# Attention and gated MLP on one core: gate taken off TensorE, V load, gate-weight load and Q evictions moved, units cut finer

## Chip, cores and metric

One core of one Trainium2 chip. The time is device microseconds of one execution. Most numbers below are medians of several executions, with the spread. A run carries a state (fast or slow). For one core, slow means more than 1.5% above the fastest run of the same kernel. The profile shows one execution of each kernel, and its span is about 1.7 us shorter than the time of that execution.

## The reference, cut to what matters

```python
x = A_x                                              # 2048 x 512, bf16
g = sigmoid((x * gate_w).sum(-1, keepdims=True))     # one number per token
a = A_ref(x, wqkv, wo)      # 32 heads of 16, causal, sliding window of 256
b = B_ref(x, w1, w3, w2)    # (silu(x @ w1) * (x @ w3)) @ w2, inner size 1376
return g * a + (1 - g) * b
```

Both branches read the same `x`.

## The kernel before

The kernel builds a list of operations, each with an engine, an assumed duration and its dependencies. It then places them in time with a small list scheduler while the program is built. What runs on the chip is a fixed order of instructions on each engine. TensorE (PE) carries everything: the projections, the score bursts (four matmuls at once, 32 rows each, into a PSUM buffer "big" of which there is only one), the products with V (PV), the MLP ("up" and "down") and the output projection. ScalarE (ACT) does one exp per burst, GpSimd (POOL) masks it, and VectorE (DVE) evicts most of the rest.

```python
# loads: the ACT queue and the SP queue
dma("x0", "SP", 3.4, ...)      # 256 rows of x
dma("k0", "ACT", 3.4, ...)     # K weights of the first 8 heads
dma("x1", "SP", 4.2, ...)
dma("q0", "ACT", 4.2, ...)
dma("v", "ACT", 6.0, lambda: w_dma(nc.scalar, wqkv_sb, A_wqkv, 2 * D, 3 * D))   # 512 KB
dma("x2", "SP", 7.5, ...); dma("x3", "SP", 8.0, ...); dma("kq", "SP", 11.0, ...)
# ... w1, w3, the rest of x, w2, wo
nc.gpsimd.dma_start(out=gwc[:], in_=gate_w.rearrange("(c p) -> p c", p=P))      # 1 KB

# gate: 16 one-column matmuls for each quarter of the tokens
def pe():                                            # in add_gate
    b = bank(key)
    for j in range(4):
        m = 4 * m4 + j
        for dc in range(NDC):
            nc.tensor.matmul(b[:, j:j + 1], lhsT=xT[:, dc, m * P:(m + 1) * P],
                             rhs=gwc[:, dc:dc + 1], start=(dc == 0), stop=(dc == NDC - 1))

# Q eviction: one half on ACT, one on DVE
bs = [Op(("ACT",) if i == 0 else ("DVE",), d, evac_q(i), [a], rel=[("g", key)], rank=-0.5)
      for i in range(2)]

# units of PE work: parts of two matmuls; a burst can be put between parts
a0, a = pe_unit(0.87, [pe(kg, w1_sb, 0), pe(kg, w1_sb, 2)], ...)   # up; V, Q, K, output alike
cuts = [0, 2, 4, 6, 8, NFC]                                        # down: parts of 2, 2, 2, 2, 3

# the scheduler may run the MLP units only in their order
if o.kind == "ffn" and not o.cont and o.seq != ffn_next:
    continue
```

The softmax here doesn't subtract the row's maximum and nothing guards it: scores larger than these inputs give would overflow.

## Time and profile before

| | before |
|---|---|
| median of 16 runs | 273.68 us (270.59 to 274.86) |
| span of the profiled execution | 270.9 us |
| PE busy | 255.8 us, 94% |
| ACT, POOL, DVE busy | 204, 150, 141 us |
| PE waits | 1.4 us for exp, 3.6 us for the V weights, 4.0 us for transposes in the tail |

The page of the profile, first the busy time, then rows that cut the span into 40 slices (the clock in tenths, the bytes moved in GB/s):

```profile
PE 255.8 (94%) x2814; PEld 126.0 (47%) x2814; DVE 140.8 (52%) x248; ACT 204.4 (75%) x161; POOL 150.2 (55%) x251
...
PEclk9889999999999999999999999999999999999995
...
GB/s 146 343 208 269 301 6 7 13 11 13 12 5 17 10 7 7 10 12 10 12 10 12 13 4 9 10 13 10 13 9 12 47 46 30 48 31 50 39 56 45
```

All waits of PE (us in total, times, longest):

```profile
PE g L423 <- DMA OT<-ocur: 4.0, 3, 2.5
PE g L284 <- DMA wqkv_sb<-in_A_wqkv_dram: 3.6, 1, 3.6
PE big L472 <- ACT edm L480: 1.4, 3, 0.8
PE g L730 <- DVE scr L96: 1.3, 1, 1.3
PE g L198 <- DMA xs<-in_A_x_dram: 0.6, 2, 0.4
PE g L239 <- DVE h L361: 0.3, 1, 0.3
```

PE is the bound, and what it loses lies at the two ends. The Trainium skill, "Perfetto Trace Analysis", section "Identifying the Most-Contended Engine", warns that matmul busy time is a poor measure of the distance to the peak. The timeline of the head (start, duration, engine, line, operation) shows the gap:

```profile
1.37 0.87 POOL L159 DMA_DIRECT2D gwc<-in_gate_w_dram  x1 [0.32 <-issue]
...
6.04 1.73 PE L239 MATMUL g<-xT,wqkv_sb 128*128 128x256 bf16 x12
...
11.39 0.96 PE L284 MATMUL g<-wqkv_sb,xT 128*128 128x512 bf16 x2 [3.63 <-DMA wqkv_sb<-in_A_wqkv_dram]
...
12.29 0.61 PE L472 MATMUL big<-qz,kt 32*128 32x512 bf16 x4
```

PE does nothing from 7.77 to 11.39 us, and the first burst (L472) comes only after that. The same head as busy time in stretches (length, busy time of PE, PEld, DVE, ACT, POOL with counts, then granted clock, DMA share, GB/s):

```profile
4.00:6.00 2.00, 1.39 (x16) 1.17 (x17) 0.91 (x3) 0.00 (x0) 0.99 (x2) 1.00 0.85 196
6.00:8.00 2.00, 1.67 (x14) 1.06 (x11) 0.81 (x2) 1.68 (x3) 0.00 (x0) 1.00 0.88 275
8.00:11.00 3.00, 0.00 (x0) 0.00 (x0) 0.58 (x2) 0.28 (x1) 0.00 (x0) 1.00 1.10 349
11.00:15.00 4.00, 3.61 (x12) 1.02 (x13) 0.69 (x1) 1.88 (x1) 0.10 (x1) 0.57 1.51 319
```

After the gap the granted clock is 0.57 on average for four microseconds. The tail, PE's timeline without the PV matmuls:

```profile
254.16 0.39 PE L472 MATMUL big<-qz,kt 32*128 32x512 bf16 x4
256.61 0.29 PE L472 MATMUL big<-qz,kt 32*128 32x256 bf16 x4 [0.76 <-ACT edm L480]
...
258.88 1.04 PE L423 MATMUL g<-xs,OT 128*128 128x512 bf16 x4 [1.22 <-DMA OT<-ocur]
260.23 0.39 PE L423 MATMUL g<-xs,OT 128*128 128x512 bf16 x1 [0.31 <-DMA OT<-ocur]
...
264.96 2.31 PE L423 MATMUL g<-xs,OT 128*128 128x512 bf16 x5 [2.48 <-DMA OT<-ocur]
```

PE waits for the attention output to be normalised and transposed by DMA, and the last five matmuls run at half clock (0.46 us each).

### The profile page before, as it was taken

The page shows a single profiled execution, that of the slowest core. Times are in us where ns is not written, and L with a number is a line of the kernel's source. Part 1 is how long each engine was busy: PE and PEld are TensorE (multiplying, and loading weights), DVE is VectorE, ACT ScalarE, POOL GpSimd, SP SyncE. Part 2 cuts the span into 40 slices and gives each one's busy share as a digit, 9 for nine tenths or more (in the row PEclk, how much of TensorE's full clock was granted, in tenths as well). Part 3 has the DMA queues.
Part 4 walks back from the last instruction along what each step waited for, and adds up shares of the span by engine and source line. Part 5 has one row for each costly group of instructions (what it writes and reads, how often), then busy time and mean ns, then how long its engine had stood idle before and what let it go on. Part 6 is the DMA issues. An engine that isn't in the chain of part 4 may idle for free.

```text
span 270.9 us, 6643 instructions
## 1 busy us (share of the span) xinstructions
PE 255.8 (94%) x2814; PEld 126.0 (47%) x2814; DVE 140.8 (52%) x248; ACT 204.4 (75%) x161; POOL 150.2 (55%) x251
## 2 busy tenths in 40 slices
PE   7499999999999999999999999999999999999853
PEld 3154555445554545545554555544554454545420
DVE  1164775575565545554736545465554656544432
ACT  3278887896988887898878978899778778867600
POOL 5036656556645666465745755576655755575620
PEclk9889999999999999999999999999999999999995
DMA  5999900000000000000000000000000111111111
GB/s 146 343 208 269 301 6 7 13 11 13 12 5 17 10 7 7 10 12 10 12 10 12 13 4 9 10 13 10 13 9 12 47 46 30 48 31 50 39 56 45
DMA packets 24750, 13.05 MB, mean 48 GB/s; under 512 B 16176, under 2 KB 24720, under 8 KB 24720
## 3 DMA queue, kind: packets, MB, share of 16 engines
q1 hardware_dynamic: 23104, 11.84, 17.4%
q10 hardware_dynamic: 1584, 0.79, 1.0%
q8 instruction: 22, 0.36, 0.6%
q0 software_dynamic: 32, 0.00, 0.2%
q14 instruction: 8, 0.07, 0.1%
HBM read 7.37 MB, written 2.10 MB: 35 GB/s over the span
## 4 chain that ended last, share of the span: by engine, by line
PE 85%; DMA 5%; ACT 4%; DVE 2%; issue 1%; SPq 0%; ACTq 0%
PE g L349 27%; PE g L395 15%; PE g L535 13%; PE big L472 11%; PE g L239 10%; PE g L423 5%; PE g L284 5%; DMA wqkv_sb<-in_A_wqkv_dram 3%; ACT edm L480 3%; DMA OT<-ocur 2%; DVE qz L257 1%; ACT ef L480 1%; DVE h L361 1%; ACT tt L356 0%; SPq L550 0%
## 5 line engine op out<-in xcount | busy, mean ns | idle before, releaser
L480 ACT ACTIVATE edm<-big 128x2048 bf16<-128x2048 f32 x64 | 116.7, 1824 | 33.5 <-PE big L472 26.7
L489 POOL TENSOR_SCALAR_AFFINE_SELECT edm<-edm 128x512 bf16<-128x512 bf16 x128 | 78.6, 638 | 68.8 <-ACT edm L480 65.4
L494 POOL TENSOR_SCALAR_AFFINE_SELECT ef<-ef 128x512 bf16<-128x512 bf16 x112 | 67.6, 636 | 39.3 <-ACT ef L480 37.9
L349 PE MATMUL g<-xT,w_sb 128*128 128x512 bf16 (+1 forms) x352 | 86.2, 380 | 0.0
L480 ACT ACTIVATE ef<-big 128x2048 bf16<-128x2048 f32 x28 | 52.6, 1877 | 10.6 <-PE big L472 9.9
L361 DVE SCALAR_TENSOR_TENSOR h<-tt,g 128x512 bf16<-128x512 bf16 (+1 forms) x44 | 30.1, 684 | 40.1 <-ACT tt L356 39.9
L349 PEld LDWEIGHTS <-w_sb 128*128 128x128 bf16 (+1 forms) x352 | 31.7, 100 | 39.0 <-issue 7.9
L395 PE MATMUL g<-w_sb,hT 128*128 128x512 bf16 (+1 forms) x176 | 42.6, 380 | 0.0
L535 PE MATMUL g<-Vaug,edm 128*128 128x17 bf16 x992 | 41.0, 170 | 0.0
L535 PEld LDWEIGHTS <-edm 128*128 128x128 bf16 x992 | 38.5, 96 | 4.1
L472 PE MATMUL big<-qz,kt 32*128 32x512 bf16 (+1 forms) x480 | 36.2, 330 | 1.5 <-ACT edm L480 1.4
L535 PE MATMUL g<-Vaug,ef 128*128 128x17 bf16 x448 | 37.2, 171 | 0.0
L535 PEld LDWEIGHTS <-ef 128*128 128x128 bf16 x448 | 35.1, 96 | 4.4 <-issue 1.1
L239 PE MATMUL g<-xT,wqkv_sb 128*128 128x512 bf16 (+1 forms) x136 | 33.2, 367 | 0.4 <-DVE h L361 0.3
L367 DVE TENSOR_TENSOR hT<-h,g 128x512 bf16<-128x512 bf16 (+1 forms) x44 | 30.1, 685 | 4.0 <-PE g L349 1.2
L356 ACT ACTIVATE tt<-g 128x512 bf16<-128x512 f32 (+1 forms) x44 | 26.0, 592 | 0.4 <-PE g L349 0.4
L395 PEld LDWEIGHTS <-hT 128*128 128x128 bf16 (+1 forms) x176 | 15.7, 98 | 20.0 <-issue 3.6
L404 DVE TENSOR_SCALAR bsb<-g,omg 128x512 bf16<-128x512 f32 x16 | 12.0, 750 | 23.0 <-PE g L395 23.0
L472 PEld LDWEIGHTS <-kt 32*128 32x128 bf16 x480 | 10.2, 91 | 29.3 <-issue 28.3
L284 PE MATMUL g<-wqkv_sb,xT 128*128 128x512 bf16 x64 | 17.7, 405 | 3.7 <-DMA wqkv_sb<-in_A_wqkv_dram 3.6
L423 PE MATMUL g<-xs,OT 128*128 128x512 bf16 x64 | 17.1, 400 | 4.0 <-DMA OT<-ocur 4.0
L430 DVE SCALAR_TENSOR_TENSOR ot<-g,gq,bsb 128x512 bf16<-128x512 f32 x16 | 11.9, 749 | 12.6 <-PE g L423 12.1
(37 smaller groups left out, 116.7 us busy)
## 6 DMA issues: line engine op xcount, KB each, us to landing
out_dram<-ot SPq DMA_DIRECT2D x16, 128.0 KB, 1.7
w_sb<-in_B_w_dram SPq DMA_DIRECT2D x2, 864.0 KB, 7.0
w_sb<-in_B_w_dram SPq DMA_DIRECT2D x1, 1280.0 KB, 6.4
xs<-in_A_x_dram SPq DMA_DIRECT2D x4, 256.0 KB, 5.8
w_sb<-in_B_w_dram SPq DMA_DIRECT2D x2, 512.0 KB, 10.0
OT<-ocur SPq DMA_TRANSPOSE x64, 2.4
wqkv_sb<-in_A_wqkv_dram SPq DMA_DIRECT2D x2, 384.0 KB, 9.2
wqkv_sb<-in_A_wqkv_dram ACTq DMA_DIRECT2D x1, 512.0 KB, 9.4
```

Source lines behind the costliest of these rows:

```text
L239: nc.tensor.matmul(b[:, 0:n], lhsT=wqkv_sb[:, dc, col0:col0 + P], rhs=xT[:, dc, t0:t1], start=(dc == 0), stop=(dc == NDC - 1))
L284: nc.tensor.matmul(b[:], lhsT=xT[:, c, m * P:(m + 1) * P], rhs=wqkv_sb[:, c, 2 * D:3 * D], start=(c == 0), stop=(c == NDC - 1))
L349: nc.tensor.matmul(b[0:fs, :], lhsT=wsb[:, dc, f * P:f * P + fs], rhs=xT[:, dc, t * 512:(t + 1) * 512], start=(dc == 0), stop=(dc == NDC - 1))
L361: nc.vector.scalar_tensor_tensor(out=tl["h1"][0:fs, :], in0=tl["tt"][0:fs, :], scalar=1.0, in1=g_tile[kg][0:fs, :], op0=ALU.add, op1=ALU.mult)
L367: nc.vector.tensor_tensor(out=h_tile[t][0:fs, f, :], in0=tl["h1"][0:fs, :], in1=g_tile[ku][0:fs, :], op=ALU.mult)
L395: nc.tensor.matmul(b[:], lhsT=h_tile[t][0:fs, f, (m % 4) * P:(m % 4 + 1) * P], rhs=w2_sb[0:fs, f, :], start=(f == 0), stop=(f == NFC - 1))
L423: nc.tensor.matmul(b[:], lhsT=OT[:, c * S + m * P:c * S + (m + 1) * P], rhs=wo_t[c // 2][:, c % 2, :], start=(c == 0), stop=(c == NDC - 1))
L472: nc.tensor.matmul(big[:, u, k * 256:k * 256 + 2 * w], lhsT=kt[32 * u:32 * u + 32, kb * P:(kb + 1) * P], rhs=qz[32 * u:32 * u + 32, :, q0: ...
L480: nc.scalar.activation(out=e[:, :, 0:2 * n], in_=tl["big"][:, :, 0:2 * n], func=ACT.Exp, scale=SCALE)
L489: nc.gpsimd.affine_select(out=tri, in_=tri, pattern=[[0, 2], [0, 2], [1, P]], compare_op=ALU.is_ge, fill=0.0, base=0, channel_multiplier=-1)
L494: nc.gpsimd.affine_select(out=tri, in_=tri, pattern=[[0, 4], [-1, P]], compare_op=ALU.is_ge, fill=0.0, base=-1, channel_multiplier=1)
L535: nc.tensor.matmul(pva[:, k, h8, :], lhsT=lhsT, rhs=Vaug[:, kp, 8 * c + h8, :], start=(bi == 0), stop=(bi == len(blocks) - 1))
```

## The change

The intent: have the V weights early, take the gate off PE, take Q evictions off ACT, and cut units so finely that there is always filler for PE. Cut to its core:

```diff
-    dma("v", "ACT", 6.0, lambda: w_dma(nc.scalar, wqkv_sb, A_wqkv, 2 * D, 3 * D))
+    dma("v", "SP", 6.5, lambda: w_dma(nc.sync, wv_sb, A_wqkv, 0, D, 2 * D))    # between x1 and x2
+    # wv_sb lies in a sixth exp buffer, which is free for exp once V is done
-    nc.gpsimd.dma_start(out=gwc[:], in_=gate_w.rearrange("(c p) -> p c", p=P))
+            if o.eng == "POOL" and not gw_done:              # while the order is written out
+                npool[0] += 1
+                if npool[0] == 9:                            # before the ninth mask
+                    nc.gpsimd.dma_start(out=w1_sb[:, :, F:F + 1], in_=gate_w.rearrange("(c p x) -> p c x", p=P, x=1))
-    # 64 gate matmuls
+            m = fs + 1 if has_z and key == kg else fs        # last chunk of w1: row 97 is the gate
+        def put(eng):
+            nc.sync.dma_start(out=zd[t:t + 1, :], in_=tl["tt"][row:row + 1, :])   # row to DRAM
+        def get(eng):
+            nc.sync.dma_start(out=st["gt"][:], in_=zd[t, :].rearrange("(j p) -> p j", p=P))  # back, as columns
-            bs = [Op(("ACT",) if i == 0 else ("DVE",), d, evac_q(i), ...
+            bs = [Op("DVE", d, evac_q(i), ...
-        ... [pe(kg, w1_sb, 0), pe(kg, w1_sb, 2)] ...         # and all other units
+        ... [pe(kg, w1_sb, i) for i in range(NDC)] ...
-        cuts = [0, 2, 4, 6, 8, NFC]
+        cuts = range(NFC + 1)
```

Left out of this print: the weights of Q, K and V in three tiles, the transposes of x in halves evicted by DVE and ACT side by side, the last w1 chunk taken fifth, Q before K for the first 512 tokens, K's first eviction allowed on ACT, and new assumed landing times.

More of the change, by code (lines that the diff above doesn't have):

```diff
@@ L58 @@
     bsb = pp.tile([P, NT, D], BF16, name="bsb")
-    gwc = pp.tile([P, NDC], BF16, name="gwc")
-    w1_sb = pp.tile([P, NDC, F], BF16, name="w1_sb")
+    w1_sb = pp.tile([P, NDC, F + 1], BF16, name="w1_sb")
     w3_sb = pp.tile([P, NDC, F], BF16, name="w3_sb")
-    wqkv_sb = pp.tile([P, NDC, 3 * D], BF16, name="wqkv_sb")
+    wk_sb = pp.tile([P, NDC, D], BF16, name="wk_sb")
+    wq_sb = pp.tile([P, NDC, D], BF16, name="wq_sb")
     eo = pp.tile([P, 4], F32, name="eo")
@@ L70 @@
     smpool = ctx.enter_context(tc.tile_pool(name="sm", bufs=3))
+    dr = ctx.enter_context(tc.tile_pool(name="dr", bufs=1, space=bass.MemoryType.DRAM))
+    zd = dr.tile([NTC, 512], F32, name="zd")
     ps = ctx.enter_context(tc.tile_pool(name="ps", bufs=1, space=bass.MemoryType.PSUM))
@@ L90, in hold @@
         refs[(pool, key)] = n
+    hold("edm", "wv", NT)
+    slot_of[("edm", "wv")] = 5
     def slot(pool, key):
@@ L108, in xt_dma, with w_dma @@
                                     in_=x2d[512 * t:512 * (t + 1), c * P:(c + 1) * P])
-    def w_dma(eng, dst, src, lo, hi):
-        eng.dma_start(out=dst[:, :, lo:hi], in_=src[:, lo:hi].rearrange("(c p) f -> p c f", p=P))
+    def w_dma(eng, dst, src, lo, hi, base=0):
+        eng.dma_start(out=dst[:, :, lo:hi],
+                      in_=src[:, base + lo:base + hi].rearrange("(c p) f -> p c f", p=P))
+    wv_sb = sb.tile([P, NDC, D], BF16, name="edm5")
     land = {}
@@ L117, in dma @@
         land[name] = at
-    dma("x0", "SP", 3.4, lambda: x_dma(0, 0))
-    dma("k0", "ACT", 3.4, lambda: w_dma(nc.scalar, wqkv_sb, A_wqkv, D, D + P))
-    dma("x1", "SP", 4.2, lambda: x_dma(0, 1))
-    dma("q0", "ACT", 4.2, lambda: w_dma(nc.scalar, wqkv_sb, A_wqkv, 0, P))
-    dma("v", "ACT", 6.0, lambda: w_dma(nc.scalar, wqkv_sb, A_wqkv, 2 * D, 3 * D))
-    dma("x2", "SP", 7.5, lambda: x_dma(1, 0))
+    dma("x0", "SP", 4.1, lambda: x_dma(0, 0))
+    dma("k0", "ACT", 3.6, lambda: w_dma(nc.scalar, wk_sb, A_wqkv, 0, P, D))
+    dma("x1", "SP", 4.9, lambda: x_dma(0, 1))
+    dma("q0", "ACT", 4.2, lambda: w_dma(nc.scalar, wq_sb, A_wqkv, 0, P))
+    dma("v", "SP", 6.5, lambda: w_dma(nc.sync, wv_sb, A_wqkv, 0, D, 2 * D))
+    dma("x2", "SP", 7.3, lambda: x_dma(1, 0))
     dma("x3", "SP", 8.0, lambda: x_dma(1, 1))
-    dma("kq", "SP", 11.0, lambda: (w_dma(nc.sync, wqkv_sb, A_wqkv, D + P, 2 * D),
-                                   w_dma(nc.sync, wqkv_sb, A_wqkv, P, D)))
+    dma("kq", "SP", 10.5, lambda: (w_dma(nc.sync, wk_sb, A_wqkv, P, D, D),
+                                   w_dma(nc.sync, wq_sb, A_wqkv, P, D)))
     FA = 4 * P
-    dma("wa", "SP", 14.0, lambda: (w_dma(nc.sync, w1_sb, B_w1, 0, FA),
+    dma("wa", "SP", 13.8, lambda: (w_dma(nc.sync, w1_sb, B_w1, 0, FA),
                                    w_dma(nc.sync, w3_sb, B_w3, 0, FA)))
@@ L189, in add_tx, with pe, evac @@
     def add_tx(m2):
-        key = ("tx", m2)
-        hold("g", key, 1)
-        def pe():
-            tx = bank(key, BF16, (P, 2, NDC, P))
-            xs = xs_tiles[m2]
-            for j in range(2):
-                for c in range(NDC):
-                    nc.tensor.transpose(out=tx[:, j, c, :], in_=xs[:, j, c * P:(c + 1) * P],
-                                        identity=ident[:])
-        def evac(eng):
-            dst = xT[:, :, 2 * m2 * P:(2 * m2 + 2) * P].rearrange("p c (j t) -> p j c t", j=2)
-            if eng == "ACT":
-                nc.scalar.copy(out=dst, in_=g_tile[key][:])
-            else:
-                nc.vector.tensor_copy(out=dst, in_=g_tile[key][:])
-        a = Op("PE", 0.5, pe, [loads[f"x{m2}"]], acq=[("g", key)], kind="tx")
-        b = Op(("DVE", "ACT"), 0.65, evac, [a], rel=[("g", key)], rank=-1)
-        xT_op[m2] = b
+        xT_op[m2] = []
+        for half in range(2):
+            key = ("tx", m2, half)
+            hold("g", key, 1)
+            cs = slice(2 * half, 2 * half + 2)
+            def pe(key=key, half=half):
+                tx = bank(key, BF16, (P, 2, 2, P))
+                for j in range(2):
+                    for c in range(2):
+                        d0 = (2 * half + c) * P
+                        nc.tensor.transpose(out=tx[:, j, c, :], in_=xs_tiles[m2][:, j, d0:d0 + P],
+                                            identity=ident[:])
+            def evac(eng, key=key, cs=cs):
+                dst = xT[:, cs, 2 * m2 * P:(2 * m2 + 2) * P].rearrange("p c (j t) -> p j c t", j=2)
+                if eng == "ACT":
+                    nc.scalar.copy(out=dst, in_=g_tile[key][:])
+                else:
+                    nc.vector.tensor_copy(out=dst, in_=g_tile[key][:])
+            a = Op("PE", 0.25 if m2 > 1 else 0.45, pe, [loads[f"x{m2}"]], acq=[("g", key)], kind="tx")
+            xT_op[m2].append(Op("ACT" if half else "DVE", 0.55 if half else 0.36, evac, [a],
+                                rel=[("g", key)], rank=-1))
     def xdep(t0, t1):
@@ L214, in xdep @@
         for m2 in range(t0 // 256, (t1 + 255) // 256):
-            r.append(xT_op[m2] if m2 < 4 else loads["x4" if m2 < 6 else "x6"])
+            r += xT_op[m2] if m2 < 4 else [loads["x4" if m2 < 6 else "x6"]]
         return r
@@ L224, in add_proj @@
         n = t1 - t0
-        col0 = (0 if is_q else D) + c * P
         first = (c, "alloc") not in qk_tile
@@ L237, in fn @@
                 b = bank(key) if d0 == 0 else g_tile[key]
-                for dc in range(d0, d0 + 2):
-                    nc.tensor.matmul(b[:, 0:n], lhsT=wqkv_sb[:, dc, col0:col0 + P],
+                for dc in range(d0, d0 + 1):
+                    nc.tensor.matmul(b[:, 0:n], lhsT=(wq_sb if is_q else wk_sb)[:, dc, c * P:(c + 1) * P],
                                      rhs=xT[:, dc, t0:t1], start=(dc == 0), stop=(dc == NDC - 1))
@@ L261, in add_proj @@
         w = loads[("q0" if is_q else "k0") if c == 0 else "kq"]
-        a0, a = pe_unit(0.216 * NDC * n / 512, [pe(0), pe(2)], xdep(t0, t1) + [w],
+        a0, a = pe_unit(0.216 * NDC * n / 512, [pe(i) for i in range(NDC)], xdep(t0, t1) + [w],
                         acq=[("g", key)] + ([("qk", c)] if first else []), kind="proj")
@@ L265, in add_proj @@
         if is_q:
-            bs = [Op(("ACT",) if i == 0 else ("DVE",), d, evac_q(i), [a], rel=[("g", key)], rank=-0.5)
+            bs = [Op("DVE", d, evac_q(i), [a], rel=[("g", key)], rank=-0.5)
                   for i in range(2)]
@@ L269, in add_proj @@
         else:
-            bs = [Op("DVE", d, evac_k, [a], rel=[("g", key)], rank=-0.5)]
+            bs = [Op(("ACT", "DVE") if c == 0 and t0 < 512 else "DVE", d, evac_k, [a], rel=[("g", key)], rank=-0.5)]
             K_op.setdefault(c, []).append((t0, t1, bs))
@@ L282, in fn @@
                 b = bank(key) if d0 == 0 else g_tile[key]
-                for c in range(d0, d0 + 2):
+                for c in range(d0, d0 + 1):
                     nc.tensor.matmul(b[:], lhsT=xT[:, c, m * P:(m + 1) * P],
-                                     rhs=wqkv_sb[:, c, 2 * D:3 * D], start=(c == 0),
+                                     rhs=wv_sb[:, c, :], start=(c == 0),
                                      stop=(c == NDC - 1))
@@ L294, in evac @@
                 nc.vector.tensor_copy(out=Vaug[:, m, :, 0:DH], in_=src)
-        a0, a = pe_unit(0.87, [pe(0), pe(2)], xdep(m * P, (m + 1) * P) + [loads["v"]],
-                        acq=[("g", key)], kind="v")
+        a0, a = pe_unit(0.87, [pe(i) for i in range(NDC)], xdep(m * P, (m + 1) * P) + [loads["v"]],
+                        acq=[("g", key)], rel=[("edm", "wv")], kind="v")
         V_op[m] = Op("DVE", 0.66, evac, [a], rel=[("g", key)])
@@ L301, with add_gate @@
     gate_op = {}
-    def add_gate(m4):
-        key = ("z", m4)
-        hold("g", key, 1)
+    def add_gate(t, b, tl, row):
         st = {}
-        def pe():
-            b = bank(key)
-            for j in range(4):
-                m = 4 * m4 + j
-                for dc in range(NDC):
-                    nc.tensor.matmul(b[:, j:j + 1], lhsT=xT[:, dc, m * P:(m + 1) * P],
-                                     rhs=gwc[:, dc:dc + 1], start=(dc == 0), stop=(dc == NDC - 1))
-        def th(eng):
+        def put(eng):
+            nc.sync.dma_start(out=zd[t:t + 1, :], in_=tl["tt"][row:row + 1, :])
+        def get(eng):
             st["gt"] = smpool.tile([P, 4], F32, name="gt")
-            nc.scalar.activation(out=st["gt"][:], in_=g_tile[key][:, 0:4], func=ACT.Tanh, scale=0.5)
+            nc.sync.dma_start(out=st["gt"][:], in_=zd[t, :].rearrange("(j p) -> p j", p=P))
         def fin(eng):
             gt = st["gt"]
-            nc.vector.tensor_scalar(out=gq[:, 4 * m4:4 * m4 + 4], in0=gt[:], scalar1=0.5,
+            nc.vector.tensor_scalar(out=gq[:, 4 * t:4 * t + 4], in0=gt[:], scalar1=0.5,
                                     scalar2=0.5, op0=ALU.mult, op1=ALU.add)
-            nc.vector.tensor_scalar(out=omg[:, 4 * m4:4 * m4 + 4], in0=gt[:], scalar1=-0.25,
+            nc.vector.tensor_scalar(out=omg[:, 4 * t:4 * t + 4], in0=gt[:], scalar1=-0.25,
                                     scalar2=0.25, op0=ALU.mult, op1=ALU.add)
-        a = Op("PE", 0.43, pe, xdep(512 * m4, 512 * m4 + 512), acq=[("g", key)], kind="gate")
-        b = Op("ACT", 0.2, th, [a], rel=[("g", key)])
-        gate_op[m4] = Op("DVE", 0.35, fin, [b])
-        return a
+        d = Op("SP", 3.5, put, [b])
+        e = Op("SP", 4.5, get, [d])
+        gate_op[t] = Op("DVE", 0.35, fin, [e])
     h_tile, up_done = {}, {}
@@ L335, in add_up @@
         fs = fsz(f)
+        has_z = f == NFC - 1
         kg, ku, kt_, kh = ("G", t, f), ("U", t, f), ("tt", t, f), ("h1", t, f)
@@ L345, in pe @@
         def pe(key, wsb, d0):
+            m = fs + 1 if has_z and key == kg else fs
             def fn():
                 b = bank(key) if d0 == 0 else g_tile[key]
-                for dc in range(d0, d0 + 2):
-                    nc.tensor.matmul(b[0:fs, :], lhsT=wsb[:, dc, f * P:f * P + fs],
+                for dc in range(d0, d0 + 1):
+                    nc.tensor.matmul(b[0:m, :], lhsT=wsb[:, dc, f * P:f * P + m],
                                      rhs=xT[:, dc, t * 512:(t + 1) * 512],
@@ L354, in th @@
         def th(eng):
-            tl["tt"] = sb.tile([P, 512], BF16, name=f"tt{slot('tt', kt_)}")
-            nc.scalar.activation(out=tl["tt"][0:fs, :], in_=g_tile[kg][0:fs, :], func=ACT.Tanh,
+            m = fs
+            if has_z:
+                tl["tt"] = xp.tile([P, 512], F32, name="xs2")
+                m = fs + 1
+            else:
+                tl["tt"] = sb.tile([P, 512], BF16, name=f"tt{slot('tt', kt_)}")
+            nc.scalar.activation(out=tl["tt"][0:m, :], in_=g_tile[kg][0:m, :], func=ACT.Tanh,
                                  scale=0.5)
@@ L371, in add_up @@
         x = xdep(512 * t, 512 * (t + 1))
-        a0, a = pe_unit(0.87, [pe(kg, w1_sb, 0), pe(kg, w1_sb, 2)], x + [w], acq=[("g", kg)],
+        a0, a = pe_unit(0.87, [pe(kg, w1_sb, i) for i in range(NDC)], x + [w], acq=[("g", kg)],
                         kind="ffn")
-        u0, u = pe_unit(0.87, [pe(ku, w3_sb, 0), pe(ku, w3_sb, 2)], x + [w], acq=[("g", ku)],
+        u0, u = pe_unit(0.87, [pe(ku, w3_sb, i) for i in range(NDC)], x + [w], acq=[("g", ku)],
                         kind="ffn")
@@ L380, in add_up @@
         up_done.setdefault(t, []).append(e)
+        if has_z:
+            add_gate(t, b, tl, fs)
         return [a0, u0]
@@ L421, in fn @@
                 b = bank(key) if c0 == 0 else g_tile[key]
-                for c in range(c0, c0 + 2):
+                for c in range(c0, c0 + 1):
                     nc.tensor.matmul(b[:], lhsT=OT[:, c * S + m * P:c * S + (m + 1) * P],
@@ L432, in fin @@
             nc.sync.dma_start(out=out2d[m * P:(m + 1) * P, :], in_=ot[:])
-        a0, a = pe_unit(0.87, [pe(0), pe(2)], [pv_out[(c, m // 2)] for c in range(NDC)] + [loads["wo"]],
+        a0, a = pe_unit(0.87, [pe(i) for i in range(NDC)], [pv_out[(c, m // 2)] for c in range(NDC)] + [loads["wo"]],
                         acq=[("g", key)], kind="out")
@@ L583 @@
         for t0, t1 in pieces:
-            for is_q in (False, True):
+            for is_q in ((True, False) if t1 <= 512 else (False, True)):
                 a = add_proj(c, t0, t1, is_q)
@@ L590 @@
         a.need = when(0, 3 * (m // 2)) - 1.0
-    for m4 in range(NTC):
-        a = add_gate(m4)
-        a.need = 20.0 + 12 * m4
     for c in range(NDC):
@@ L606 @@
     for t in range(NTC):
-        for f in range(NFC):
+        for n, f in enumerate([0, 1, 2, 3, NFC - 1] + list(range(4, NFC - 1))):
             ffn += add_up(t, f)
-            if t and f in (1, 3, 5, 7):
-                ffn.append(add_down(4 * t - 4 + f // 2))
+            if t and n in (1, 3, 5, 7):
+                ffn.append(add_down(4 * t - 4 + n // 2))
     for m in range(NT - 4, NT):
@@ L625 @@
     free_at = {e: 0.0 for e in ("PE", "ACT", "DVE", "POOL", "SP")}
-    free_at["PE"] = 3.3
+    free_at["PE"] = 3.9
     ready = {e: [] for e in free_at}
@@ L725 @@
                     ready[x].append(u)
+    gw_done, npool = [], [0]
     with tc.manual_schedule():
@@ L734 @@
                 wo_dma()
+            if o.eng == "POOL" and not gw_done:
+                npool[0] += 1
+                if npool[0] == 9:
+                    nc.gpsimd.dma_start(out=w1_sb[:, :, F:F + 1],
+                                        in_=gate_w.rearrange("(c p x) -> p c x", p=P, x=1))
+                    gw_done.append(1)
             if o.eng == "PE":
```

## The prediction

> **What bounds the kernel now.** TensorE: the busy table gives PE 255.8 of 270.9 us (94%; ACT 204, POOL 150, DVE 141), the chain of waits is 85% PE, and the stretch table shows PE full from 20 to 255 us at clock 1.00, about 1.1 us idle. The losses lie at the ends:
>
> - Head. The timeline has PE idle from 7.77 to 11.39 us; the waits put 3.6 us on the DMA of the V weights (9.4 us to land, ACT queue). The first score burst stands behind those V matmuls and starts at 12.28. Then the granted clock is 0.50 until about 14.6 (V matmuls 0.43 us apart, not 0.22), about 1.5 us more. The Trainium skill, "TensorE: Matmul & The Clock Gate", Part 1, says the clock falls to half after an idle window of about 3.4 us; this trace agrees.
> - Tail. The last burst starts at 254.2, the span ends 16.7 us later, but PE has only some 6.4 us of warm work (two PV units of 1.2, two output pairs of 1.7, the burst). Twice it waits for PV, normalise, transpose by DMA (4.4 and 3.1 us); the last five matmuls run at clock 0.50.
> - Gate. 64 one-column matmuls at about 25 ns (a PV unit's 48 take 1.20 us): 1.6 us of a full PE.
>
> **What the change does.**
>
> 1. V weights go third on the SP queue, ahead of half of x and other weights. By the GB/s row the 1.3 MB up to their end had passed by about 7.7 us, so V should land near 7.7 and the first burst start near 8.5, with no cold stretch. Counting work up to the fourth burst, I estimate 4.1 us saved (3 to 5).
> 2. The gate becomes a 97th row of the last w1 chunk, free on PE: 1.6 us. Its detour through DRAM blocks the SP queue a few us per quarter, before anybody needs it: 0.
> 3. Units are cut into single matmuls: same PE work, as many bursts. Filler per burst becomes about ten 512-column matmuls (2.2 us + 0.33 of burst), still just longer than exp 1.88 plus handoff (2.3). The gain is at the tail: the instruction order puts two down projections (22 matmuls, 4.75 us) after the last burst, where PE was waiting. PE work there becomes 11.0 us, plus 0.5 of wait and 3.6 from last matmul to end: 15.2 instead of 16.7, and 4.75 less before it: 5.8 us saved.
> 4. Q evictions leave ACT for DVE (12 us more at 52% busy), a sixth exp buffer: off the critical path, 0.
>
> **Sum.** 4.1 + 1.6 + 5.8 = 11.5 us, less 0.5 for small new waits: span about 260, time about 262.
>
> Predicted 262.0 us, range 258.5 to 266.0; faster by over 2%: 0.94, within 2%: 0.05, slower: 0.01.
>
> **What would show it.** Head: no PE wait on the V weights above 1 us, first burst at 8 to 9.5 us, clock 1.00 from 4 to 20 us. Gate: its matmul group gone. Middle: PE idle below 2 us. Tail: last burst near 243.5, from it to the end 15 to 16 us, clock 1.00 until the last matmul.
>
> **What would make it wrong.** V weights landing after 9 us; x or the w1 chunk now late, so the head's wait moves instead of going; exp falling behind the shorter fillers; the SP queue's blocked transposes holding the first outputs; the last output still waiting 2 us or more for its transpose. Each costs 1 to 3 us; it takes three of them to lose the 2%.

## The result

| | before | after |
|---|---|---|
| median | 273.68 us (16 runs, 270.59 to 274.86) | 258.21 us (11 runs, 257.90 to 258.98) |
| profiled span | 270.9 us | 256.7 us |
| PE busy | 255.8 us, 94% | 250.7 us, 98% |
| first burst / last burst starts | 12.29 / 256.61 us | 8.36 / 242.10 us |

The ratio is 0.945, with a 95% interval of 0.9425 to 0.9475. A ratio here is the mean time of one kernel's fast runs over that of the other's of the same rounds, so it isn't quite the ratio of the medians. The runs also lie closer together, 1.1 us apart instead of 4.3.

The page after:

```profile
PE 250.7 (98%) x2750; PEld 122.9 (48%) x2750; DVE 150.9 (59%) x266; ACT 194.9 (76%) x143; POOL 150.0 (58%) x251
...
PEclk9999999999999999999999999999999999999999
```

All waits of PE after:

```profile
PE g L738 <- DVE scr L101: 1.3, 1, 1.3
PE g L208 <- DMA xs<-in_A_x_dram: 0.6, 2, 0.5
PE g L293 <- DMA edm<-in_A_wqkv_dram: 0.4, 1, 0.4
```

The waits for exp and for transposes are gone, and the V wait is 0.4 us. The head after, as timeline and in stretches:

```profile
7.82 0.61 PE L293 MATMUL g<-edm,xT 128*128 128x512 bf16 x2 [0.44 <-DMA edm<-in_A_wqkv_dram]
8.36 0.39 PE L482 MATMUL big<-qz,kt 32*128 32x512 bf16 x4
```

```profile
4.00:6.00 2.00, 1.37 (x17) 1.15 (x18) 0.74 (x3) 0.59 (x1) 0.00 (x0) 1.00 1.14 305
6.00:8.00 2.00, 1.56 (x14) 1.09 (x13) 1.71 (x5) 0.96 (x2) 0.00 (x0) 1.00 1.10 351
8.00:11.00 3.00, 2.89 (x30) 1.46 (x28) 1.64 (x4) 2.20 (x2) 0.25 (x1) 1.00 1.11 332
11.00:15.00 4.00, 4.00 (x30) 1.79 (x31) 2.22 (x4) 3.54 (x4) 2.21 (x4) 1.00 1.25 289
```

Note the last column of the first row: 305 GB/s between 4 and 6 us, where the kernel before moved 196. Nothing in the prediction explains that. The tail after, where two down projections (L405) fill the place of the waits:

```profile
242.10 0.29 PE L482 MATMUL big<-qz,kt 32*128 32x256 bf16 x4
243.54 2.54 PE L405 MATMUL g<-w_sb,hT 128*128 128x512 bf16 x11
247.13 1.89 PE L433 MATMUL g<-xs,OT 128*128 128x512 bf16 x8
248.85 2.54 PE L405 MATMUL g<-w_sb,hT 128*128 128x512 bf16 x11
251.23 1.89 PE L433 MATMUL g<-xs,OT 128*128 128x512 bf16 x8
```

**Where the 14.2 us of span went.** The two orders have different work between the same bursts, so start times alone mislead. For each stretch between bursts I subtract the PE work that the instruction order has in it, at unit costs read from the traces: 0.2163 us for a 512-column matmul (11 of them take 2.38 us in the chain of waits), 0.0252 for a PV or gate matmul (48 in about 1.2 us), 0.33 for a burst, and 0.055 for a transpose of 128 columns, an estimate from their spacing. What remains I call lost. The units are a little too small, so some loss remains even where PE is never idle; only differences count.

| stretch | lost before | lost after | won |
|---|---|---|---|
| start to 4th burst | 9.92 | 5.14 | 4.78 |
| 4th to 20th burst | 2.33 | 1.59 | 0.74 |
| 20th to last burst | 8.44 | 7.04 | 1.40 |
| last burst to end | 9.29 | 3.63 | 5.66 |
| gate matmuls (64 x 0.0252) | | | 1.61 |
| sum | | | 14.19 |

This closes on the two spans (270.9 - 256.7 = 14.2). Medians differ by 15.5, because the profiled execution of before took 272.57 us, 1.1 under its median.

### The profile page after: what moved, and what is told of

It is laid out like the page before. It is cut to its first block, busy times and chain, and to the rows that moved or that the text cites. A ratio compares the mean times of both kernels' runs of the same rounds, so it can differ in the third digit from the quotient of the medians.

```text
span 256.7 us, 6546 instructions
## 1 busy us (share of the span) xinstructions
PE 250.7 (98%) x2750; PEld 122.9 (48%) x2750; DVE 150.9 (59%) x266; ACT 194.9 (76%) x143; POOL 150.0 (58%) x251
## 4 chain that ended last, share of the span: by engine, by line
PE 95%; DMA 2%; DVE 1%; SPq 0%; issue 0%
PE g L352 31%; PE g L405 16%; PE g L545 14%; PE big L482 12%; PE g L248 11%; PE g L293 6%; PE g L433 6%; DMA edm<-in_A_wqkv_dram 2%; SPq L106 0%; DVE ot L440 0%; DVE Vaug L303 0%; PE g L208 0%
## 5 line engine op out<-in xcount | busy, mean ns | idle before, releaser
L352 PE MATMUL g<-xT,w_sb 128*128 128x512 bf16 (+2 forms) x352 | 88.8, 381 | 0.0
L352 PEld LDWEIGHTS <-w_sb 128*128 128x128 bf16 (+2 forms) x352 | 31.5, 100 | 38.2 <-issue 9.1
L369 DVE SCALAR_TENSOR_TENSOR h<-tt,g 128x512 bf16<-128x512 bf16 x40 | 27.4, 685 | 34.8 <-ACT tt L364 34.3
L405 PE MATMUL g<-w_sb,hT 128*128 128x512 bf16 (+1 forms) x176 | 42.9, 380 | 0.0
L545 PE MATMUL g<-Vaug,edm 128*128 128x17 bf16 x992 | 41.7, 170 | 0.0
L545 PE MATMUL g<-Vaug,ef 128*128 128x17 bf16 x448 | 37.8, 171 | 0.0
L266 DVE TENSOR_SCALAR qz<-g,maskEO 128x512 bf16<-128x512 f32 (+1 forms) x34 | 22.9, 714 | 5.3 <-PE g L248 5.0
L405 PEld LDWEIGHTS <-hT 128*128 128x128 bf16 (+1 forms) x176 | 15.9, 98 | 20.6 <-issue 4.1
L364 ACT ACTIVATE tt<-g 128x512 bf16<-128x512 f32 x40 | 23.7, 592 | 0.1
L248 PE MATMUL g<-xT,wq_sb 128*128 128x512 bf16 (+1 forms) x68 | 17.4, 368 | 0.0
L293 PE MATMUL g<-edm,xT 128*128 128x512 bf16 x64 | 16.8, 379 | 0.4 <-DMA edm<-in_A_wqkv_dram 0.4
L248 PE MATMUL g<-xT,wk_sb 128*128 128x512 bf16 (+1 forms) x68 | 16.8, 366 | 0.0
```

Source lines behind the costliest of these rows:

```text
L248: nc.tensor.matmul(b[:, 0:n], lhsT=(wq_sb if is_q else wk_sb)[:, dc, c * P:(c + 1) * P], rhs=xT[:, dc, t0:t1], start=(dc == 0), stop=(dc = ...
L293: nc.tensor.matmul(b[:], lhsT=xT[:, c, m * P:(m + 1) * P], rhs=wv_sb[:, c, :], start=(c == 0), stop=(c == NDC - 1))
L352: nc.tensor.matmul(b[0:m, :], lhsT=wsb[:, dc, f * P:f * P + m], rhs=xT[:, dc, t * 512:(t + 1) * 512], start=(dc == 0), stop=(dc == NDC - 1))
L364: nc.scalar.activation(out=tl["tt"][0:m, :], in_=g_tile[kg][0:m, :], func=ACT.Tanh, scale=0.5)
L369: nc.vector.scalar_tensor_tensor(out=tl["h1"][0:fs, :], in0=tl["tt"][0:fs, :], scalar=1.0, in1=g_tile[kg][0:fs, :], op0=ALU.add, op1=ALU.mult)
L405: nc.tensor.matmul(b[:], lhsT=h_tile[t][0:fs, f, (m % 4) * P:(m % 4 + 1) * P], rhs=w2_sb[0:fs, f, :], start=(f == 0), stop=(f == NFC - 1))
```

## The experiments

Twelve kernels ran, in three calls. All outputs are right. Each call had its own runs of the kernel before: medians 272.77, 273.22 and 273.13 us. Kernels named "a" and "c" add parts to the kernel before, and those named "b" undo parts of the changed kernel. In the first call three of the eleven runs of before were slow (274.6 to 274.9 us) and left out. In the other two calls runs of before of up to 275.0 us count as fast, because the fastest run there was slower; so the first call's gains may be understated, by about 0.8 us if the three are put back. A cost "by ratio" is a difference of two ratios times 273.4 us. Each interval is about 0.003 to either side, so such a difference is good to about 1.1 us. The traced spans differ a little from that, because a trace is one execution.

### First call: single parts, on the kernel before

**a1: V on the SP queue.** The PE order is unchanged.

```diff
-    dma("v", "ACT", 6.0, lambda: w_dma(nc.scalar, wqkv_sb, A_wqkv, 2 * D, 3 * D))
+    dma("v", "SP", 6.0, lambda: w_dma(nc.sync, wqkv_sb, A_wqkv, 2 * D, 3 * D))
```

> The kernel before, with the V weights alone moved to third place on the SP queue; the PE order is unchanged. Theory (the head's loss is this one late DMA plus the slow clock after its gap): first burst near 8.4 us instead of 12.3, clock 1.00 from 11 to 15 us, V wait below 0.7 us, time 4 to 5.5 us shorter. Rival (the head needs the split transposes and single-matmul units as well): less than 2 us shorter, with a new PE wait before 20 us.

Measured: 271.60 us (269.05 to 272.28), ratio 0.998 (0.9945 to 1.0017). This is a miss, and my theory fell. The profiled execution was the fastest of the six. In its head the clock stayed at 1.00, but V still landed only at 9.5 us and the first burst came at 10.06:

```profile
4.00:6.00 2.00, 1.49 (x16) 1.23 (x17) 0.91 (x3) 0.11 (x1) 0.99 (x2) 1.00 0.71 167
6.00:8.00 2.00, 1.50 (x12) 1.06 (x11) 0.80 (x2) 1.78 (x3) 0.00 (x0) 1.00 0.87 256
8.00:11.00 3.00, 1.48 (x9) 0.52 (x10) 0.58 (x2) 0.55 (x2) 0.00 (x0) 1.00 1.10 347
```

From the same place in the same queue V landed at 7.8 us in the changed kernel. So something else slows the transfers, as at 4 to 6 us before (167 and 196 GB/s, against 305). The only other early transfer that the change removes is the gate-weight load at 1.37 us.

**a2: both Q evictions on DVE.**

```diff
-            bs = [Op(("ACT",) if i == 0 else ("DVE",), d, evac_q(i), [a], rel=[("g", key)], rank=-0.5)
+            bs = [Op("DVE", d, evac_q(i), [a], rel=[("g", key)], rank=-0.5)
```

> The kernel before, with both Q evictions on DVE instead of one on ACT. The prediction on record says 0. New theory: the three PE waits for exp between 30 and 60 us of before (1.4 us in all) come from Q evictions that sit before an exp on ACT, so they vanish and the time falls by 1 to 1.5 us. Rival: no change (within 0.5 us), the waits move elsewhere.

Measured: 272.77 us, ratio 1.003 (0.9993 to 1.0059), so no gain in time. In the trace the losses between 4th and last burst fall from 10.77 to 10.16 us and the PE waits for exp from 1.4 to 0.8 us, but V happened to land later there (first burst at 13.43). Inconclusive alone; b2 below asks again without that noise.

**a3: units cut into single matmuls.**

```diff
-        cuts = [0, 2, 4, 6, 8, NFC]
+        cuts = range(NFC + 1)
         # and [pe(0), pe(2)] -> [pe(i) for i in range(NDC)] in all other units
```

> The kernel before, with only the units cut into single matmuls. Its PE order holds 33 down-projection matmuls back behind the last burst (before: none). Theory (the gain is the tail alone): last burst 6 to 8 us earlier, PE full from it until the last matmul, time 5 to 6.5 us shorter, head as before. Rival (granularity feeds exp all along): PE idle between 20 and 240 us falls by more than 1 us as well.

Measured: 267.85 us, ratio 0.984 (0.9798 to 0.9879), 4.4 us by ratio (the expectation had 5 to 6.5) and 5.6 in the traces. The last burst starts at 248.96 instead of 256.61, and the loss after it falls from 9.29 to 3.60 us. Between the 4th and the last burst the loss is 10.73 us, against 10.77 before. So the finer units won the tail and nothing in the middle; the rival is out.

**c1: the head's gap filled with 16 idle matmuls.** The V wait stays; only the clock is kept up.

```diff
+                if m == 0 and d0 == 0:
+                    for _ in range(16):
+                        nc.tensor.matmul(b[:], lhsT=warm[:, 0:P], rhs=warm[:], start=True, stop=True)
                 for c in range(d0, d0 + 2):      # the first V unit
```

> The kernel before, with 16 matmuls on a zero tile put into the head's PE gap, ahead of the first V matmul; the V wait stays. Theory (the gap costs its own length plus a slow clock after it): V still lands near 11.4 us, but the clock stays 1.00 from 11 to 15 us and the time falls by about 1.5 us, and the runs spread less. Rival (the slow clock there is hidden by later waits): no change within 0.4 us.

Measured: 271.18 us (270.10 to 272.35), ratio 0.997 (0.993 to 1.0002). V is still late, but the clock stays up:

```profile
8.00:11.00 3.00, 3.00 (x16) 1.37 (x14) 0.97 (x2) 0.49 (x2) 0.00 (x0) 1.00 1.10 348
11.00:15.00 4.00, 4.00 (x37) 2.08 (x35) 1.82 (x3) 2.71 (x2) 0.76 (x2) 1.00 1.46 316
```

The 4th burst starts 1.67 us earlier than before (19.84 against 21.51). V landed 0.30 us earlier here (11.05 against 11.35), so about 1.4 us remain for the clock, near the 1.5 expected. The time shows 0.9 us by ratio, and its interval just reaches 1. The runs lie 2.3 us apart, those of before 4.5. So the trace shows the gap's second cost, and the times do not contradict it.

### Second call: the gate-weight load, the queue, the Q evictions

**a6: a1, and the gate weights loaded after the second mask.**

```diff
-    nc.gpsimd.dma_start(out=gwc[:], in_=gate_w.rearrange("(c p) -> p c", p=P))
+            if o.eng == "POOL":
+                npool[0] += 1
+                if npool[0] == 3:
+                    nc.gpsimd.dma_start(out=gwc[:], in_=gate_w.rearrange("(c p) -> p c", p=P))
```

> The kernel before, with V on the SP queue as in a1 and, in addition, the load of the gate weights (1 KB in 512 pieces of 2 bytes, from the POOL queue) moved out of the first 2 us to behind the first two masks; PE order unchanged. V landed at 9.5 us in a1 but at 7.8 us in the changed kernel from the same place in the same queue. Theory: this tiny load slows all transfers of the head. Then V lands near 7.8, first burst near 8.4, and the time is 4 to 5 us under before, with runs as close together as the changed kernel's (about 1 us). Rival (the split weight tiles or something else makes V early): as a1, V at 9.5 and 0.5 to 1 us under before.

Measured: 267.15 us (266.73 to 267.53), ratio 0.976 (0.9731 to 0.9795). That is 6.5 us under before by ratio, more than the 4 to 5 expected, where a1 had 0.5. The runs lie 0.8 us apart.

```profile
4.00:6.00 2.00, 1.27 (x18) 1.12 (x19) 0.84 (x2) 0.01 (x1) 0.00 (x0) 1.00 1.14 316
6.00:8.00 2.00, 1.77 (x14) 1.07 (x12) 0.91 (x2) 1.69 (x3) 0.00 (x0) 1.00 1.10 346
8.00:11.00 3.00, 3.00 (x32) 1.72 (x32) 2.13 (x4) 2.70 (x3) 0.59 (x1) 1.00 1.11 332
```

The rate between 4 and 6 us is 316 GB/s instead of 167. The first burst starts at 8.02 us, PE doesn't wait for V any more, and the loss up to the 4th burst is 4.42 us, less than in the changed kernel. A load of 1 KB, 512 numbers of 2 bytes each, was holding up more than a megabyte of others.

**b6: the changed kernel with the gate weights loaded at the start again.** The PE order is unchanged.

```diff
-                if npool[0] == 9:
+                if False:
+    nc.gpsimd.dma_start(out=w1_sb[:, :, F:F + 1],                     # in the preamble
+                        in_=gate_w.rearrange("(c p x) -> p c x", p=P, x=1))
```

> The changed kernel with only the load of the gate weights back at the start of the program, same PE order. Theory: V lands near 9.5 instead of 7.8 us, 1.5 to 3 us over the changed kernel, and a wider spread of runs. Rival: no change within 0.5 us.

Measured: 261.50 us (260.23 to 262.43), ratio 0.955 (0.9515 to 0.9591), 2.8 us by ratio over the changed kernel, and the spread doubles to 2.2 us. PE waits 1.9 us for V (0.4 in the changed kernel). The rates fall as in a1:

```profile
4.00:6.00 2.00, 1.75 (x16) 1.51 (x17) 0.73 (x4) 0.59 (x1) 0.99 (x2) 1.00 0.63 140
6.00:8.00 2.00, 1.55 (x15) 1.16 (x13) 1.61 (x5) 0.96 (x2) 0.00 (x0) 1.00 0.83 252
```

In steps of 1 us the loss is a hole after 5 us. The first line is b6, the second the changed kernel:

```profile
5.00:6.00 1.00, 0.89 (x10) 0.74 (x9) 0.73 (x4) 0.59 (x1) 0.00 (x0) 1.00 0.28 40
5.00:6.00 1.00, 0.60 (x9) 0.56 (x10) 0.35 (x2) 0.56 (x1) 0.00 (x0) 1.00 1.04 292
```

All six kernels with the early load have this hole (40 to 80 GB/s between 5 and 6 us), and the seven with the late load, b3's disturbed trace aside, don't (208 to 313). The packet records in the traces put the small load's own 16 packets of 64 bytes around the hole, between 4.7 and 8.2 us in these six, and half of them take over 0.36 to 0.49 us, depending on the run. Issued late, from the same queue, the median is 0.044 us in every run. So the small size alone doesn't make the load slow. In the hole the DMA engines are busy for only 0.28 of the time, and POOL does nothing, so POOL's memset, which the edit shifts too, isn't what fills it.

This pair settles that the early load is the cause, in both directions. The Trainium skill, "DMA: Bandwidth & Descriptors", section "Specifications", gives 512 bytes as the least transfer that runs at line rate, and says that below it the engine reads, modifies and writes. These runs show more: the small load cuts the rate of the large ones. Why the load is slow when it is early, and whether the 2-byte pieces or the software queue of POOL matter, no run here separates.

**b1: the changed kernel with V on the ACT queue again.** The PE order is unchanged.

```diff
-    dma("v", "SP", 6.5, lambda: w_dma(nc.sync, wv_sb, ...
+    dma("v", "ACT", 6.5, lambda: w_dma(nc.scalar, wv_sb, ...
```

> The changed kernel with the V weights back on the ACT queue, same PE order, gate weights still late. Theory: V lands late again, between 9 and 11.5 us; each us is lost once[...]: 2 to 5 us over the changed kernel, all of it before the fourth burst. Rival (with the gate load gone V is early from either queue): under 1 us.

Measured: 261.90 us, ratio 0.955 (0.9514 to 0.9592), 2.8 us by ratio over the changed kernel, as expected. In the traces 3.5 of the 3.7 us lie before the 4th burst. V takes 8.1 us from issue to landing instead of 5.9, issued at 1.90 and 1.82 us. The skill's "Issuing engines are not separate DMA queues" (same page) says that loads from different engines run on the same 16 engines and interleave. That agrees: on its own queue V shares with what SP has issued, on SP's it goes ahead of it. With V on ACT, SP's third load (x2) landed at 7.42 us and V at 10.01; in the changed kernel V landed at 7.77 and x2 at 8.53. PE waited 3.0 us here, and the clock fell (0.68 from 12 to 16 us), though the wait was shorter than the window of about 3.4 us that the prediction cites.

**b2: the changed kernel with one Q eviction on ACT again.**

```diff
-            bs = [Op("DVE", d, evac_q(i), ...
+            bs = [Op(("ACT",) if i == 0 else ("DVE",), d, evac_q(i), ...
```

> The changed kernel with one of the two Q evictions back on ACT (the order shifts in places from the 38th burst on). Theory: some of the middle's 2.1 us comes back as PE waits for exp behind a Q eviction: 0.5 to 1.5 us over the changed kernel, between the fourth and the last burst. Rival: no change within 0.4 us.

Measured: 260.45 us (260.31 to 260.89), ratio 0.952 (0.9489 to 0.955), 1.9 us by ratio over the changed kernel, a little above the band. The loss between 20th and last burst is 9.23 us instead of 7.04, and PE waits for exp again:

```profile
PE big L482 <- ACT edm L490: 1.0, 2, 0.9
...
PE big L482 <- ACT ef L490: 0.6, 1, 0.6
```

So Q evictions do cost PE time from ACT, at 75% busy. There is one exp per burst and one PSUM buffer for bursts, so an ACT job placed before an exp delays the next burst. The edit also shifts the order from the 38th burst on, so the 1.9 us belong to the eviction's place and to the order that follows from it; the two can't be parted here.

### Third call: units, gate, the sum, and the filler's place

**b3: the changed kernel with units in pairs again.**

```diff
-        cuts = range(NFC + 1)
+        cuts = [0, 2, 4, 6, 8, NFC]
         # and pairs in all other units
```

> The changed kernel with its units cut in pairs again, as before. Its order ends like that of the kernel before: no down projection behind the last burst. Theory (the units' gain is the filled tail): from last burst to end PE has about 5 us of work and loses about 5.7 us more than the changed kernel; 5.5 to 7 us over it. Rival (other parts of the change had filled the tail or feed exp as well): under 3 us.

Measured: the five fast runs took 265.05 to 265.76 us, ratio 0.972 (0.9691 to 0.9751), so 7.4 us by ratio over the changed kernel, a little above the band. It is the largest part of the change. The sixth, profiled execution took 958 us: 512-column matmuls started 1.28 us apart until about 400 us and 0.84 us apart after that, instead of 0.22, while ACT's exps kept their 1.88 us. Its trace holds no clock record, unlike every other trace, so the 1.00 that is listed for its clock is no measurement. No other execution did so. It's put aside as a disturbance, so b3 has no trace to compare.

**b4: the changed kernel with the gate on PE again, its weights loaded late.**

```diff
-        has_z = f == NFC - 1
+        has_z = False          # and the 64 one-column matmuls of the kernel before
```

> The changed kernel with the gate back as 64 one-column matmuls on TensorE (its weights still loaded late, so the head is left alone). Theory: 64 x 25 ns = 1.6 us over the changed kernel, up to 2.2 if the order suffers. Rival (hidden in waits): under 0.5 us.

Measured: 261.37 us, ratio 0.9565 (0.9536 to 0.9595), 3.1 us by ratio over the changed kernel, more than expected. In the trace 1.6 us are PE work, 0.7 lie before the 4th burst and 1.4 after the 20th, where PE waits 0.8 us for exp. The 0.7 is as much as V landed later in this trace (8.49 us, not 7.77), which the gate doesn't explain. The gate units take places in the order, and the waits suggest that the order around them is worse; which displaced unit costs what is open.

**a8: the kernel before with V on SP, late gate weights, Q on DVE and single-matmul units.** The edits of a6, a2 and a3 together.

```diff
+ a6 + a2 + a3
```

> The kernel before with four parts together: V on the SP queue, gate weights loaded late, Q evictions on DVE, single-matmul units. Left out of the change: the gate row, the split transposes, the split weight tiles and the order of the chunks. Theory (these four and the gate are all of it): 1.6 us over the changed kernel, so 259.5 to 260.5 us, runs within 1 us of each other. Rival (the parts left out matter): over 261.5 us.

Measured: 261.06 us (260.26 to 262.22), ratio 0.956 (0.953 to 0.9597). That is outside both bands of the expectation, half a microsecond over the first, and the runs lie 2.0 us apart, not 1. By ratio it is 3.1 us over the changed kernel, just what b4 says the gate is worth. So the four parts and the gate account for the whole change within the error of about 1.1 us, and the split transposes, the three weight tiles and the order of chunks need not be worth anything. Alone, a6 and a3 gave 6.5 and 4.4 us, sum 10.9; together with Q they give 11.9.

**a9: a6 with the last two down projections held until after the last burst**, units still in pairs.

```diff
+                if o.kind == "ffn" and not o.cont and o.seq >= len(ffn) - 2 and bursts_left > 0:
+                    continue
```

> The kernel of a6 (267.2 us) with the last two down projections held until after the last burst, the units still in pairs. Theory: the tail's wait of 5.7 us is filled, but between the 88th and the last burst the fillers shrink to less than an exp takes, so PE waits there for exp: net gain 1 to 3 us over a6. Rival (only the place of the filler counts): 5 to 6 us.

Measured: 270.29 us, ratio 0.989 (0.9855 to 0.9923): 3.4 us by ratio slower than a6, not faster. A miss in sign. PE's wait for transposes in the tail fell (3.6 to 1.1 us), but waits for exp grew more (0.8 to 5.2 us among the last bursts), and the clock was at half from 244.8 to 248.2 and from 251.6 to 255.1 us, among those bursts. From 238 us to the end:

```profile
PE big L471 <- ACT edm L479: 5.2, 3, 2.1
PE g L422 <- DMA OT<-ocur: 1.1, 2, 0.9
...
```

So the filler that is kept for the tail must not be missing between the last bursts. In a9's order the gaps behind the 88th and 89th burst hold only half a PV unit and two output matmuls, less than the exp of 1.88 us takes. The changed kernel's order has a whole PV unit and four output matmuls behind the 88th burst, ten down matmuls behind each of the 89th and 90th, and still two whole down projections behind the last one. That the finer cut is what frees this filler is what a3 shows, and b3's time agrees; how the scheduler comes to save it up over the earlier bursts I only argue, from gaps of ten matmuls where the kernel before often has eleven. Nothing measured beat the changed kernel, and no trace pointed to a version that would.

## Why the prediction was right or wrong

The direction was right, and the order of the parts was nearly right. The time, 258.21 us, came out 3.8 us under the 262.0 foreseen and 0.3 us below the low end of the range.

- **Head, foreseen 4.1, found 4.8 in the trace.** The size was good and the reason was half wrong. I read the V load as late because of its queue, and saw the first burst at 8.5 (8.36 came). But a1 shows the queue alone to be worth 0.5 us; with the gate weights loaded late as well it is 6.5 (a6). My estimate of 7.7 us for V's landing came from the bytes passed in a trace in which the small load was still slowing them, and in a1 V landed at 9.5. That it fitted the changed kernel was luck: the diff line that moves the gate load stood before me, and I costed it as nothing.
- **Clock after the gap.** Right in size: c1 shows about 1.4 us for it in the trace, foreseen 1.5. The window of about 3.4 us that the prediction cites fits this gap of 3.6 us, but not the tail of the same trace: there the clock fell at 264.1 us, 1.6 us into a wait of 2.5.
- **Gate, foreseen 1.6.** Its PE work is 1.6 us; undoing it costs 3.1 (b4). The rest lies in V's landing and in PE waits after the 20th burst; that the disturbed order makes these waits is argued, not shown.
- **"4. Q evictions leave ACT for DVE ...: off the critical path, 0."** This step failed. b2 shows 1.9 us. I judged ACT by its average of 75%, but before each burst there is an exp, and PE's waits for exp stood in the waits of the kernel before (1.4 us).
- **"less 0.5 for small new waits".** This failed with it. In the middle, losses didn't grow by 0.5 but fell by 2.1 us (0.74 + 1.40). That is the largest missing term.
- **Tail, foreseen 5.8, found 5.7.** Right in size and mechanism (a3's trace; b3 agrees in time, without a trace). But "the last burst starts at 254.2" was a misreading: that is the last but one, and the last starts at 256.61. The stretch from last burst to end was 14.3 us and became 14.6, not 16.7 to 15.2; what was won is the work that now fits into it. a9 shows what I had not seen: moving filler there is worth nothing unless the gaps between the last bursts stay filled.
- **Time over span.** I added about 2 us to the span; the changed kernel's runs lie 1.5 over its profiled span.

## What to carry to other kernels

Look at every transfer of the head, small ones too: a 1 KB load of 2-byte numbers issued at 1.4 us cost as much as the wrong queue for a 512 KB load (2.8 us each when undone), and on the page it showed only as a lower rate of the others. When a saturated engine waits at the end of a kernel, keep independent work for that place, but cut it small enough that the gaps before are still filled. An engine at 75% busy can be on the critical path where a single buffer makes the next step wait for it, as ACT was in b2.

## What the Trainium skill lacked or had wrong

- "DMA: Bandwidth & Descriptors": it says that transfers under 512 bytes are slow themselves, but not that they slow the others. Here 512 numbers of 2 bytes, loaded from the POOL queue at 1.4 us, cut the rate of all transfers between 4 and 6 us from 305 to 140 GB/s (changed kernel and b6) and from 316 to 167 (a6 and a1).
- "DMA: Bandwidth & Descriptors", section "Issuing engines are not separate DMA queues": it says that issuing on several engines only saves the sequencer's time. For the rate of all transfers that fits here (285, 339 and 344 GB/s in the stretches of b1's head from 4 to 11 us, 305, 351 and 332 in the changed kernel's), but not for a single load: V took 8.1 us on the ACT queue and 5.9 us in third place on SP.
- "TensorE: Matmul & The Clock Gate": the rule of no idle gap above about 3.4 us is too mild as a limit for a single gap. In b1 the wait was 3.0 us and in the tail of the kernel before the longest was 2.5 us, and the clock fell to half in both. In a1's tail it fell at 257.3 us with no wait above 1.2 us in the 3.4 us before, while a wait of 2.0 us in a1's head left it at 1.00. So the length of one gap doesn't decide it here.
- No page I read has a whole execution like the one of 958 us in b3, with 512-column matmuls 1.28 us and later 0.84 us apart and no clock record in the trace.
